# A written first-stage order made anew, and conversion stages dealt to slots by a table

## The chip, the cores and the metric

One core of a Trainium2 chip runs the whole program. The metric is device time in microseconds (us) of one execution, taken as the median of several runs; less is better. The core has five engines with queues of their own: TensorE (PE; its weight loads are shown apart, PEld), VectorE (DVE), ScalarE (ACT), GpSimd (POOL), and SyncE (SP), whose queue issues the DMA transfers. Each engine takes its instructions in the order in which they were written, and waits when one of them needs something that is not there yet.

## What is computed

Three layers follow one another, cut here to what matters:

```python
# 1. attention, both ways, for 4 batches x 8 heads (512 rows, 32 states, 64 wide)
a  = softmax(0.125 * x @ state.T);   xread = a @ state
a2 = softmax(0.125 * state @ x.T);   sread = a2 @ x
x  = rows of [xread, sread]                   # 2304 x 512
# 2. first layer pair: 2048 wide, leaky, w_in and w_out come as float64
h = x @ w_in;  g = max(h, 0) + alpha * min(h, 0);  x = g @ w_out
# 3. eight experts, 1024 wide, with a gate normalized 8 times by rows and columns
P = exp(x @ w_gate - max);  8 times: P /= rowsum; P /= colsum; P *= N / E
out = sum over e of P[:, e] * (relu(x @ w1[e]) @ w2[e])
```

The result is wanted in float32, so each large product is made of three: every operand is split into a high and a low part (`h`, `l`), and high by high, high by low and low by high are added in PSUM.

## The kernel before

The 2048 columns of layer 2 are cut into eight units of 256. A unit's weights come as four raw pieces of float64. A piece goes through `to_f32`, a generator of three stages: stage 1 takes the exponent field (VectorE `y` L122, ScalarE `raw` L125 and `y` L126), stage 2 puts the mantissa together (VectorE L128, ScalarE L132 and L133, GpSimd sum L134), stage 3 merges the sign (VectorE L136). Then `split_w` makes the high half on ScalarE (L151) and the low half on GpSimd (L152), and `load_next` issues the load of a later raw piece into the buffer that has come free; there are three.

Attention and layer 2 are not kept apart. For the first two units the input side is folded: `v_part` multiplies the small states with the unit's weights (`pv`, L481), and its halves are evicted by ScalarE (L491) and VectorE (L494) into V; `first_layer` multiplies V with the attention weights (`ph`, L567), then come the negative part on ScalarE (L572), the leak on VectorE (L575), the halves on ScalarE (L580) and GpSimd (`gl`, L581); `second_layer` multiplies with w_out (`po`, L599), and an accumulate adds it to `acc` (L612 on VectorE, or a copy on ScalarE for unit 0).

The order of this first stage is written out by hand in `PLAN`, a list of 280 steps; `start` takes one step of the named generator for each word:

- `x0` to `x3`: `read_x`, the forward attention of a batch: scores `psc` (L257, 8 narrow products of 64 columns each, 16 records, for each half), softmax on VectorE, ScalarE and GpSimd, transposes `pat` (L289) and `pst` (L301).
- `s0` to `s3`: `read_state`, the other direction: transposes `pa` (L326), products `psr` (L335).
- `cUJ`: the conversion of piece J of unit U; `vUPJ`: a `v_part`; `hUCF`, `oUCD`: layer 1 and layer 2 blocks of unit U; `tB`: halves of a state; `b`: a constant.
- `w`: five idle products of `ones` by `ones` (`warm`, L1318, 10 records, since each float32 product is recorded twice), read by nobody.

All engines but SP run this list in the order in which it was written. Behind it, `run` walks through the remaining units: `program` alternates layer 1 of one chunk with layer 2 of the chunk before, and after each block `slot()` gives every lane of helper work one turn; a unit has 28 slots, and a block of six products of 512 columns fills one. The lane `w` holds `weights(u + 1)`, which converts the next unit's pieces while unit u is multiplied, and the lane `v` makes V as soon as the first two pieces are split. A generator that yields k is left alone for k slots. The last two units are interleaved, and there the code takes the rest of `weights(7)` at once, ahead of unit 7's first block:

```python
if (u, c) == (U1 - 1, 0):
    while (u, NPIECE - 1) not in split:
        advance("w")
```

The third layer (`experts`) follows with an order of its own, from about 412 us on.

Of the kernel before, what the change touches and what calls it, by code (L numbers as in the profile page):

```python
# [39 lines left out]
EPS = 1e-9  # L40
CUT = (1, 2, 0)
PLAN = """
c00 x0 t0 x0 c00 x1 w x0 x0 t1 x0 x0 x0 c01 x1 c02 x0 c00 s0 c01
c02 x0 x0 c01 c00 c01 t3 x0 x0 t2 x1 s0 x1 c02 v001 v000 s0 v001 c02 s0
v000 c03 s0 x1 v010 s0 x1 x1 x1 b c03 c10 h000 v010 c03 w c10 s0 x1 h000
c03 v011 v011 s1 x1 h001 c11 x1 x1 s1 x2 x2 w h000 c11 x2 x2 s1 x2 x2
x2 s1 x2 c10 h011 s1 c12 h001 h001 s1 c10 h011 c11 x2 h011 h010 s1 h010 c12 o002
x2 c11 h010 x2 o001 x2 x3 o001 x3 o003 o002 c13 o013 x3 x3 s2 x3 x3 o013 v101
x3 o003 o011 o011 v100 v101 o000 o000 s2 c12 v100 c13 v110 h101 x3 c13 o010 h101 c12 v110
c13 h100 h110 h100 h110 h101 v111 s2 h100 o010 o012 s2 h111 v111 h111 s2 h021 o102 s2 h110  # L50
o012 o100 o102 h111 h020 x3 o101 o100 h021 s2 o111 o110 s3 o101 h020 c20 o111 c20 o110 x3
o103 h020 h121 h021 x3 s3 h120 o103 x3 o112 s3 h120 c21 h121 o021 s3 o021 c22 o023 h030
c21 o023 o112 s3 c20 o113 h121 s3 o022 h030 o113 h120 h031 o022 c22 o020 o123 h031 s3 o122
o020 h031 c21 h030 h131 o121 h040 c20 o123 o122 o121 c21 c22 h131 h130 o120 h130 o030 o120 v201
o032 h131 o030 c23 h040 v201 h040 h130 o032 o033 v211 o033 o031 h140 o131 h040 o130 o031 o131 c23
v211 o040 o130 h140 c23 v210 v210 v200 o041 o041 c22 o132 o040 h140 o133 v200 o132 c23 h140 o133
"""
SCALE = 0.125

# [2 lines left out]
def body(ctx: ExitStack, tc: tile.TileContext, xt_in, xn_in, stb, stk, wd, ws, alpha, wgate, out):  # L62
# [8 lines left out]
    first = ExitStack()  # L71
# [10 lines left out]
    def f32(t):  # L82
        return t.bitcast(F32)
# [18 lines left out]
    def load_w(u, j):  # L102

        raw_t[u, j] = rawp.tile([P, 512], U64, tag="raw", name=f"raw{u}_{j}")
        nc.sync.dma_start(out=raw_t[u, j], in_=wd[u, j])

    def load_next(u, j):

        i = u * NPIECE + j + 3
        if i < U1 * NPIECE:  # L110
            load_w(i // NPIECE, i % NPIECE)

    def to_f32(u, j):

        w = raw_t[u, j].bitcast(I32).rearrange("p (n two) -> p n two", two=2)
        s = raw_t[u, j].bitcast(U16).rearrange("p (n four) -> p n four", four=4)
        lo_w, hi_w = w[:, :, 0], w[:, :, 1]  # L120
        y = rawp.tile([P, 512], F32, tag="y", name=f"y{u}_{j}", bufs=2)
        nc.vector.tensor_scalar(  # L122
            out=y.bitcast(I32), in0=hi_w, scalar1=16, scalar2=0x7FFF, op0=ALU.logical_shift_right, op1=ALU.bitwise_and
        )
        nc.scalar.activation(out=lo_w, in_=lo_w.bitcast(U32), func=AF.Copy, scale=2.0**-29)  # L125
        nc.scalar.activation(out=y, in_=y.bitcast(I32), func=AF.Relu, bias=rebias)  # L126
        yield
        nc.vector.scalar_tensor_tensor(  # L128
            out=lo_w, in0=s[:, :, 2], scalar=8.0, in1=lo_w, op0=ALU.mult, op1=ALU.add
        )  # L130

        nc.scalar.activation(out=y, in_=y, func=AF.Relu, scale=-1.0, bias=full)  # L132
        nc.scalar.activation(out=y.bitcast(I32), in_=y, func=AF.Copy, scale=-float(1 << 19), bias=4095.0 * (1 << 19))  # L133
        nc.gpsimd.tensor_tensor(out=lo_w, in0=y.bitcast(I32), in1=lo_w, op=ALU.add)  # L134
        yield
        nc.vector.scalar_tensor_tensor(  # L136
            out=lo_w, in0=hi_w, scalar=-0x80000000, in1=lo_w, op0=ALU.bitwise_and, op1=ALU.bitwise_or
        )
        src_t[u, j] = f32(lo_w)

    def split_w(u, j):
        if j % 2 == 0:

            for x, w in zip("hl", (wh_t, wl_t), strict=True):
                t = wp.tile([P, 2, 512], F32R, tag=("ws", "w2")[j // 2] + x, name=f"w{x}{u}_{j}")
                w[u, j], w[u, j + 1] = t[:, 0], t[:, 1]
                if j == 0:
                    w[u] = t
        split.add((u, j))
        src = src_t[u, j]  # L150
        nc.scalar.activation(out=wh_t[u, j], in_=src, func=AF.Copy)  # L151
        nc.gpsimd.tensor_tensor(out=wl_t[u, j], in0=src, in1=f32(wh_t[u, j]), op=ALU.subtract)  # L152
# [1146 lines left out]

    def weights(u, converted=0, first=5):  # L1300

        yield first
        for j in range(NPIECE):
            if j >= converted:
                for _ in to_f32(u, j):
                    yield 2
                yield 1
            split_w(u, j)
            load_next(u, j)
            yield 1  # L1310

    warm_ps = ps_o.tile([P, P], F32, tag="o", name="warm")
# [64 lines left out]
    def run(program):  # L1377
        for kind, u, c in program:
            if kind == 1:
# [11 lines left out]
                if c == 0 and 2 <= u < U1 - 1:  # L1391
                    lanes["w"].append(weights(u + 1, 0, 0 if u == U1 - 2 else 1))
                    lanes["v"].append(make_v(u + 1))
# [162 lines left out]
```

## Time and profile before

| | us |
|---|---|
| median of 3 runs | 1828.98 (1828.03 to 1837.77) |
| the profiled execution | 1835.02 |
| its span, first to last instruction | 1833.2 |
| TensorE busy | 1779.6 (97%) |
| VectorE busy | 1507.6 (82%) |
| GpSimd busy | 1250.8 (68%) |
| ScalarE busy | 736.9 (40%) |
| chain that ended last, on TensorE | 69% |

The page gives busy shares over the whole span; a stretch can look quite different. The views below are the windows (busy time of every engine in a stretch, with the granted clock of TensorE as a share of 2.4 GHz, so that 0.50 is 1.2 GHz and values between are a mix), the timeline of one engine (each line a run of like instructions, with the idle time before it and what ended it in brackets), and the waits (who waited for whom, with the total, the number of times and the longest). Products overlap on TensorE, so what a product costs is the distance from its start to the next one's, not its duration.

### The profile page before, as it was taken

How to read it: one execution, taken by the hardware profiler on the slowest of the kernel's cores; microseconds unless marked ns; L12 is line 12 of the kernel's file. 1: busy time of each engine (PE TensorE's matmuls, PEld its weight loads, DVE VectorE, ACT ScalarE, POOL GpSimd, SP SyncE). 2: the span in 40 equal slices, each digit the busy share in tenths (PEclk: the TensorE clock that was granted, in tenths of full speed). 3: DMA queues.
4: the chain of work that ended last, by engine and by line, in shares of the span. 5: the costliest groups of instructions: out<-in, count | busy, mean ns of one | idle time of the engine just before them, and what ended most of it. 6: DMA issues, size and time to landing. Idle time of an engine off the chain costs nothing.

```text
span 1833.2 us, 28679 instructions
## 1 busy us (share of the span) xinstructions
PE 1779.6 (97%) x9893; PEld 1649.8 (90%) x9893; DVE 1507.6 (82%) x2317; ACT 736.9 (40%) x1386; POOL 1250.8 (68%) x1289
## 2 busy tenths in 40 slices
PE   7999999899999999999999999999999999999998
PEld 7888888678888888888889999999999999999998
DVE  6656788776999999999987777777788888788777
ACT  6767667644234334433332222222223233232332
POOL 4345555566667777776747777777776898777775
PEclk8899999999999999999999999999999999999999
DMA  5211111114568898888887777677777787988884
GB/s 202 69 53 58 58 47 58 43 67 173 218 243 328 331 326 310 315 320 309 293 305 290 256 269 262 250 258 253 261 275 256 270 307 275 334 297 305 314 306 158
DMA packets 153008, 427.16 MB, mean 233 GB/s; under 512 B 17296, under 2 KB 34192, under 8 KB 152864
## 3 DMA queue, kind: packets, MB, share of 16 engines
q1 hardware_dynamic: 152864, 425.34, 64.0%
q8 instruction: 79, 1.29, 0.3%
q14 instruction: 65, 0.53, 0.1%
HBM read 302.28 MB, written 122.99 MB: 232 GB/s over the span
## 4 chain that ended last, share of the span: by engine, by line
PE 69%; DVE 16%; DMA 4%; issue 4%; POOL 4%; ACT 3%; SPq 1%; DVEq 0%; POOLq 0%; ACTq 0%
PE pm L1074 23%; PE py L901 11%; PE px L901 7%; PE pz L901 7%; PE po L599 7%; PE po L1219 4%; PE ph L567 4%; DVE oa L1241 2%; DVE wz L851 2%; DVE g2l L924 2%; PE psc L257 1%; DVE c L908 1%; POOL w2l L723 1%; DMA kept_bs<-wz 1%; DMA kept_a_h<-wah 1%
## 5 line engine op out<-in xcount | busy, mean ns | idle before, releaser
L1080 DVE TENSOR_TENSOR m<-pm,m 128x768 f32<-128x768 f32 (+1 forms) x427 | 377.6, 886 | 125.0 <-PE pm L1074 124.8
L1074 PE MATMUL pm<-formgh,wz 128*128 128x384 f32 (+1 forms) x1134 | 212.6, 322 | 0.4 <-DVE m L1080 0.4
L1005 POOL TENSOR_TENSOR formgh<-mid,formgh 128x384 fp32r<-128x384 f32 (+1 forms) x126 | 121.2, 962 | 105.2 <-ACT formgh L1004 105.1
L901 PE MATMUL px<-rB,wah 128*128 128x384 f32 (+1 forms) x768 | 188.8, 328 | 3.6 <-DVE g2l L924 3.4
L901 PE MATMUL py<-rT,wsh 128*128 128x384 f32 (+1 forms) x768 | 188.5, 328 | 2.3 <-DVE u L908 2.3
L1074 PEld LDWEIGHTS pm<-formgh,wz 128*128 128x128 f32 x1134 | 186.7, 188 | 0.7 <-issue 0.7
L723 POOL TENSOR_TENSOR w2l<-rw,w2h 128x512 fp32r<-128x512 f32 x64 | 87.3, 1385 | 128.9 <-ACT w2h L721 118.9
L923 ACT ACTIVATE g2h<-c 128x384 fp32r<-128x384 f32 x96 | 50.5, 526 | 305.5 <-DVE c L908 305.5
L1219 PE MATMUL po<-w2l,g2h 128*128 128x512 f32 x384 | 153.1, 399 | 0.0
L1219 PE MATMUL po<-w2h,g2h 128*128 128x512 f32 x384 | 152.3, 397 | 0.0
L1219 PE MATMUL po<-w2h,g2l 128*128 128x512 f32 x384 | 150.7, 392 | 0.1
L901 PEld LDWEIGHTS px<-rB,wah 128*128 128x128 f32 x768 | 135.8, 188 | 11.6 <-DVE g2l L924 5.8
L901 PEld LDWEIGHTS py<-rT,wsh 128*128 128x128 f32 x768 | 136.0, 188 | 5.7 <-DVE u L908 2.7
L1015 POOL TENSOR_TENSOR T<-mid,mid 128x384 f32<-128x384 f32 (+1 forms) x126 | 118.1, 960 | 30.8 <-DVE mid L989 29.5
L1004 ACT ACTIVATE formgh<-mid 128x384 fp32r<-128x384 f32 (+1 forms) x126 | 63.0, 500 | 176.6 <-DVE mid L989 135.0
L1241 DVE SCALAR_TENSOR_TENSOR oa<-po,pr,oa 128x512 f32<-128x512 f32 x168 | 124.2, 739 | 9.8 <-PE po L1219 9.2
L581 POOL TENSOR_TENSOR gl<-r,gh 128x512 fp32r<-128x512 f32 x64 | 86.8, 1364 | 61.1 <-ACT gh L580 39.1
L989 DVE SCALAR_TENSOR_TENSOR mid<-mid,pb 128x384 f32<-128x384 f32 (+1 forms) x192 | 122.7, 639 | 6.6
L901 PE MATMUL py<-rT,wsl 128*128 128x384 f32 (+1 forms) x384 | 125.7, 327 | 0.0
L1074 PE MATMUL pm<-formgl,w2h 128*128 128x384 f32 (+1 forms) x504 | 121.2, 323 | 4.5 <-POOL formgl L1005 2.7
L901 PE MATMUL px<-rB,wal 128*128 128x384 f32 (+1 forms) x384 | 125.3, 326 | 0.0
L1015 POOL TENSOR_TENSOR formgl<-T,formgl 128x384 fp32r<-128x384 f32 (+1 forms) x126 | 121.5, 964 | 1.6 <-ACT formgl L1022 1.5
(251 smaller groups left out, 5084.5 us busy)
## 6 DMA issues: line engine op xcount, KB each, us to landing
wz<-kept_bs SPq DMA_DIRECT2D x126, 512.0 KB, 8.1
kept_bs<-wz SPq DMA_DIRECT2D x64, 512.0 KB, 5.9
wsh<-kept_as_h SPq DMA_DIRECT2D x64, 512.0 KB, 3.6
wsl<-kept_as_l SPq DMA_DIRECT2D x64, 512.0 KB, 5.9
wah<-kept_a_h SPq DMA_DIRECT2D x64, 384.0 KB, 2.9
wal<-kept_a_l SPq DMA_DIRECT2D x64, 384.0 KB, 4.2
w2h<-kept_b_h SPq DMA_DIRECT2D x63, 384.0 KB, 6.4
w2l<-kept_b_l SPq DMA_DIRECT2D x63, 384.0 KB, 7.0
```

The source lines that it names most:

```text
L567: nc.tensor.matmul(ps, lhsT=w, rhs=x, start=(i == 0), stop=(i == len(terms) - 1))
L581: nc.gpsimd.tensor_tensor(out=lo, in0=r, in1=f32(hi), op=ALU.subtract)
L599: nc.tensor.matmul(bank, lhsT=w, rhs=x, start=first_of, stop=last_of)
L723: nc.gpsimd.tensor_tensor(out=lo[:, i], in0=src[:, i], in1=f32(hi[:, i]), op=ALU.subtract)
L901: nc.tensor.matmul(bank[b], lhsT=w[:, k * P:(k + 1) * P], rhs=xf[:, j, k, :], start=(first and i == 0), stop=(i == 5), skip_group_check=True,)
L989: nc.vector.scalar_tensor_tensor(out=out, in0=src, scalar=0.0, in1=pb[:, e % 2, h * n:(h + 1) * n], op0=ALU.max, op1=ALU.mult)
L1005: nc.gpsimd.tensor_tensor(out=lo, in0=out, in1=f32(hi), op=ALU.subtract)
L1015: nc.gpsimd.tensor_tensor(out=out, in0=x, in1=y, op=ALU.subtract)
L1074: nc.tensor.matmul(ps[:, q, :n], lhsT=w[:, q * P:(q + 1) * P], rhs=x, start=(j == 0), stop=(j == 2))
L1080: nc.vector.tensor_tensor(out=mm[g][name], in0=ps[:, :, :n], in1=mm[g][name], op=ALU.add)
L1219: nc.tensor.matmul(ps, lhsT=x[:, f, t * P:(t + 1) * P], rhs=w[:, f, :], start=(i == 0), stop=(i == 3 * NF - 1))
L1241: nc.vector.scalar_tensor_tensor(out=a, in0=ps, scalar=p, in1=a, op0=ALU.mult, op1=ALU.add)
```

## The change

`PLAN` is another list of the same steps: each word stands in it as often as before, but for `w`, of which there are 7 instead of 3. Two rows of the 17 show its form:

```diff
-c00 x0 t0 x0 c00 x1 w x0 x0 t1 x0 x0 x0 c01 x1 c02 x0 c00 s0 c01
+w w t0 x0 x0 w x0 t1 c00 x0 x0 x0 w x0 c01 w s0 x0 w x1
...
-v211 o040 o130 h140 c23 v210 v210 v200 o041 o041 c22 o132 o040 h140 o133 v200 o132 c23 h140 o133
+v201 h140 o131 o121 o133 c22 h040 v201 o132 o133 v210 o040 c23 o041 o132 o130 h140 c22 v210 o130
+c23 o041 o040 h140
```

`weights`, which serves units 3 to 7, now fills a table `due` from slot numbers to functions and walks through it one slot at a time. Within a piece the stages stand at slots 0, 2 and 5 (before: 0, 2 and 4), the split at slot 7 (before: 5), which is slot 1 of the next piece; a piece still begins every six slots. `converted` is 0 in every call. `first` is 1, and 0 for unit 7; before, `yield 0` and `yield 1` began at the same slot, in the table 0 begins one slot earlier.

```diff
     def weights(u, converted=0, first=5):

-        yield first
+        due, at = {}, first
         for j in range(NPIECE):
             if j >= converted:
-                for _ in to_f32(u, j):
-                    yield 2
-                yield 1
-            split_w(u, j)
-            load_next(u, j)
+                stages = to_f32(u, j)
+                for k in (0, 2, 5):
+                    due[at + k] = lambda stages=stages: next(stages, None)
+                at += 6
+            else:
+                at += 1
+
+            def last(j=j):
+                split_w(u, j)
+                load_next(u, j)
+
+            due[at + 1 if j >= converted else at - 1] = last
+        for t in range(max(due) + 1):
+            if t in due:
+                due[t]()
             yield 1
```

Since lines were added, line numbers of the kernel after are higher by 1 from `PLAN` on and by 11 behind `weights`. In the rows below, names carry the program's buffer numbers behind the last underscore.

TensorE at the head of the list (`psc` scores, `warm` idle products, `pat` and `pst` transposes, `pv` V). Before:

```order
L257 MATMUL psc_0_147<-xt_0_108 128x64 x8
L257 MATMUL psc_1_160<-xt_0_108,xt_1_111 128x64 x8
L257 MATMUL psc_0_173<-xt_0_124 128x64 x8
L1318 MATMUL warm<-ones 128x128 x5
L257 MATMUL psc_1_212<-xt_0_124,xt_1_127 128x64 x8
L289 MATMUL pat_0_247<-ident,early_101 128x128 x4
L289 MATMUL pat_1_254<-ident,early_101 128x128 x4
L301 MATMUL pst_0_276<-ident,sc_0_191 128x128 x2
L301 MATMUL pst_0_276<-ident,sc_1_201 128x128 x2
L301 MATMUL pst_1_285<-ident,sc_0_191 128x128 x2
```

After:

```order
L1329 MATMUL warm<-ones 128x128 x10
L258 MATMUL psc_0_157<-xt_0_108 128x64 x8
L258 MATMUL psc_1_166<-xt_0_108,xt_1_111 128x64 x8
L1329 MATMUL warm<-ones 128x128 x20
L258 MATMUL psc_0_235<-xt_0_124 128x64 x8
L290 MATMUL pat_0_254<-ident,early_101 128x128 x4
L290 MATMUL pat_1_261<-ident,early_101 128x128 x4
L258 MATMUL psc_1_280<-xt_0_124,xt_1_127 128x64 x8
L302 MATMUL pst_0_297<-ident,sc_0_192 128x128 x2
L302 MATMUL pst_0_297<-ident,sc_1_198 128x128 x2
```

Ten idle products now stand ahead of the first scores and twenty behind the first two score blocks, where one run of five stood behind the third; the fourth score block has moved behind `pat`.

VectorE in a plain unit, the same place in each of units 2 to 5 (`r` the leak, `raw` the merge of stage 3, `acc` an accumulate, `y` stage 1). Before:

```order
L575 SCALAR_TENSOR_TENSOR r_1_0_1928<-r_1_0_1928,beta,ph_1_0_1921 128x512
L136 SCALAR_TENSOR_TENSOR raw_0_1657<-raw_0_1657 128x512
L575 SCALAR_TENSOR_TENSOR r_1_1_1938<-r_1_1_1938,beta,ph_1_1_1931 128x512
L612 TENSOR_TENSOR acc_708<-po_0_0_1942,acc_708 128x512
L122 TENSOR_SCALAR y_1_1968<-raw_1_1754 128x512
```

After:

```order
L576 SCALAR_TENSOR_TENSOR r_1_0_1948<-r_1_0_1948,beta,ph_1_0_1941 128x512
L576 SCALAR_TENSOR_TENSOR r_1_1_1958<-r_1_1_1958,beta,ph_1_1_1951 128x512
L137 SCALAR_TENSOR_TENSOR raw_0_1701<-raw_0_1701 128x512
L613 TENSOR_TENSOR acc_591<-po_0_0_1961,acc_591 128x512
L123 TENSOR_SCALAR y_1_1982<-raw_1_1796 128x512
```

The merge now stands behind the second leak instead of between the two.

VectorE ahead of unit 7's first block (`v` the eviction of V, `raw_3` and `y_3` the last piece). Before:

```order
L575 SCALAR_TENSOR_TENSOR r_2_0_3183<-r_2_0_3183,beta,ph_2_0_3176 128x512
L494 TENSOR_TENSOR v_767<-pv_0_0_3187,v_767 64x512
L494 TENSOR_TENSOR v_766<-pv_0_0_3187,v_766 64x512
L136 SCALAR_TENSOR_TENSOR raw_2_2957<-raw_2_2957 128x512
L575 SCALAR_TENSOR_TENSOR r_2_1_3203<-r_2_1_3203,beta,ph_2_1_3196 128x512
L494 TENSOR_TENSOR v_766<-pv_0_1_3216,v_766 64x512
L494 TENSOR_TENSOR v_767<-pv_0_1_3216,v_767 64x512
L122 TENSOR_SCALAR y_3_3236<-raw_3_3066 128x512
L128 SCALAR_TENSOR_TENSOR raw_3_3066<-raw_3_3066 128x512
```

After:

```order
L576 SCALAR_TENSOR_TENSOR r_2_0_3203<-r_2_0_3203,beta,ph_2_0_3196 128x512
L137 SCALAR_TENSOR_TENSOR raw_2_2995<-raw_2_2995 128x512
L576 SCALAR_TENSOR_TENSOR r_2_1_3214<-r_2_1_3214,beta,ph_2_1_3207 128x512
L495 TENSOR_TENSOR v_667<-pv_0_0_3217,v_667 64x512
L495 TENSOR_TENSOR v_666<-pv_0_0_3217,v_666 64x512
L123 TENSOR_SCALAR y_3_3236<-raw_3_3100 128x512
L495 TENSOR_TENSOR v_666<-pv_0_1_3245,v_666 64x512
L495 TENSOR_TENSOR v_667<-pv_0_1_3245,v_667 64x512
L129 SCALAR_TENSOR_TENSOR raw_3_3100<-raw_3_3100 128x512
```

The second leak and the first step of the last piece have moved ahead, each by one eviction of V; from the `raw_3` row of L128 on the order of VectorE is the same in both, and that of the other engines from this place on as well.

## Rows read from the trace of the kernel before

**Rows 1.** Windows: PE, PEld, DVE, ACT, POOL busy (instructions), granted clock, DMA share, GB/s.

```profile
30.00:84.40 54.40, 47.86 (x253) 42.72 (x253) 36.73 (x66) 38.56 (x72) 20.83 (x17) 0.75 0.25 81
84.40:162.10 77.70, 77.70 (x425) 66.26 (x424) 45.11 (x84) 54.95 (x107) 30.19 (x25) 1.00 0.14 45
```

**Rows 2.** Timeline of TensorE, front: start, us, operation, operands, count, idle before.

```profile
5.03 3.65 PE L257 MATMUL psc<-xt 128*128 128x64 f32 x16 [5.03 <-DMA xt<-in_xt_dram]
8.47 3.62 PE L257 MATMUL psc<-xt,xt 128*128 128x64 f32 x16
...
15.30 2.45 PE L1318 MATMUL warm<-ones 128*128 128x128 f32 x10
17.54 3.51 PE L257 MATMUL psc<-xt,xt 128*128 128x64 f32 x16
...
27.17 0.58 PE L481 MATMUL pv<-wl,sth 128*128 128x256 f32 x1 [1.89 <-ACT early L307]
```

**Rows 3.** Timeline of TensorE, dense part of the list.

```profile
103.26 1.89 PE L335 MATMUL psr<-a2s,xn 128*128 128x64 f32 x16
104.96 0.48 PE L599 MATMUL po<-gl,wh 128*128 128x512 f32 x1
...
106.43 0.40 PE L567 MATMUL ph<-al,ah 128*128 128x512 f32 x1
...
107.82 0.60 PE L289 MATMUL pat<-ident,early 128*128 128x128 f32 x4
108.17 0.48 PE L599 MATMUL po<-gl,wh 128*128 128x512 f32 x1
```

**Rows 4.** Windows of 10 us, columns as in rows 1.

```profile
30.00:40.00 10.00, 7.22 (x33) 6.55 (x33) 9.43 (x16) 9.08 (x16) 3.81 (x4) 0.67 0.28 96
...
50.00:60.00 10.00, 8.04 (x42) 7.50 (x42) 5.49 (x14) 7.32 (x14) 2.55 (x2) 0.69 0.18 54
...
70.00:80.00 10.00, 9.16 (x58) 7.99 (x58) 5.88 (x10) 7.87 (x17) 5.63 (x5) 0.89 0.46 159
80.00:90.00 10.00, 10.00 (x45) 8.55 (x45) 4.58 (x10) 5.71 (x14) 1.05 (x1) 0.77 0.00 0
```

**Rows 5.** Timelines of ScalarE, VectorE, TensorE: V's evictions, first layer-1 block.

```profile
29.05 2.41 ACT L491 ACTIVATE ah<-pv 64x512 fp32r<-64x512 f32 x4
...
30.27 2.81 DVE L494 TENSOR_TENSOR al<-pv,ah 64x512 fp32r<-64x512 f32 x4 [1.51 <-ACT ah L491]
...
39.15 0.77 PE L567 MATMUL ph<-al,ah 128*128 128x512 f32 x1
```

**Rows 6.** Waits of SP's queue, 0 to 160: total us, times, longest.

```profile
SPq L105 <- POOL wl L152: 62.6, 10, 20.4
SPq L231 <- PE psr L335: 57.5, 12, 16.6
```

**Rows 7.** Timeline of VectorE in a unit; waits of TensorE, 160 to 345.

```profile
211.75 1.78 DVE L136 SCALAR_TENSOR_TENSOR raw<-raw 128x512 int32<-128x512 int32 x1 [0.90 <-POOL raw L134]
...
214.10 0.68 DVE L612 TENSOR_TENSOR acc<-po,acc 128x512 f32<-128x512 f32 x1
...
PE po L599 <- DVE acc L612: 3.1, 5, 0.6
PE po L599 <- POOL gl L581: 1.1, 4, 0.3
```

**Rows 8.** Last units: windows, timelines of TensorE, VectorE and GpSimd.

```profile
345.00:372.00 27.00, 21.86 (x91) 17.15 (x90) 17.48 (x25) 16.40 (x28) 17.18 (x18) 0.87 0.18 68
...
354.02 0.60 PE L567 MATMUL ph<-ah,v 128*128 128x512 f32 x1 [1.85 <-DVE v L494]
...
366.57 0.50 PE L599 MATMUL po<-gl,wh 128*128 128x512 f32 x1 [3.10 <-DVE acc L612]
...
360.35 0.69 DVE L136 SCALAR_TENSOR_TENSOR raw<-raw 128x512 int32<-128x512 int32 x1 [4.26 <-POOL raw L134]
...
359.01 1.30 POOL L134 TENSOR_TENSOR raw<-y,raw 128x512 int32<-128x512 int32 x1 [3.81 <-ACT y L133]
```

More of the change, by code (lines that the diff above doesn't have):

```diff
@@ L42 @@
 PLAN = """
-c00 x0 t0 x0 c00 x1 w x0 x0 t1 x0 x0 x0 c01 x1 c02 x0 c00 s0 c01
[L44 to L55, printed above, removed]
@@ L56 @@
-v211 o040 o130 h140 c23 v210 v210 v200 o041 o041 c22 o132 o040 h140 o133 v200 o132 c23 h140 o133
+w w t0 x0 x0 w x0 t1 c00 x0 x0 x0 w x0 c01 w s0 x0 w x1
+c00 c01 x0 x0 c02 c01 c00 c00 x1 c01 c02 x0 x0 x1 x1 s0 s0 x1 x1 x1
+v001 x1 v000 v001 w c03 v000 c02 x1 b c03 h001 x1 c02 s0 h001 t2 h000 h001 x1
+x1 h000 h010 c03 h000 s0 c10 s0 c03 c10 c11 x2 h011 h010 c10 c11 h011 s0 c11 o000
+o002 x2 o003 h010 t3 h011 c10 s1 o002 c11 x2 x2 o000 s1 x2 v010 x2 o003 s1 o001
+x2 v010 o013 s1 v101 x2 s1 o010 o013 o001 v101 v100 s1 c12 c13 v100 h100 h100 x2 c13
@@ new lines @@
+h101 s1 h101 o012 h100 c12 v011 o010 h110 v011 c12 c13 h101 x2 o011 c12 x2 h110 h111 o012
+x2 c13 h110 h021 x3 h111 x3 h111 o011 s2 o102 x3 x3 s2 x3 o101 x3 h020 s2 o102
+v111 s2 x3 o101 o110 x3 c21 v111 o103 h020 s2 o100 o110 x3 x3 c21 o111 h021 h020 c20
+o100 s2 h030 h021 o111 o103 c22 x3 h031 s2 o023 s3 o023 o113 x3 o113 s3 h031 h030 o021
+v110 o021 s3 o112 s3 o020 h030 o020 o112 o022 h031 v110 c20 h121 h120 o032 o022 h121 s3 c21
+s3 h121 o031 h120 o030 h120 o031 o032 s3 o123 h131 h040 c20 o123 c20 o030 h131 h130 c21 h130
@@ L57 @@
+o033 h131 c22 o122 h130 o033 o120 o120 h040 v200 o122 v200 v211 h140 h040 c23 v211 o121 c23 o131
+v201 h140 o131 o121 o133 c22 h040 v201 o132 o133 v210 o040 c23 o041 o132 o130 h140 c22 v210 o130
+c23 o041 o040 h140
 """
```

## The prediction

> **What bounds the kernel now.** TensorE does, nearly everywhere: it is busy 97% of the span, and the chain that ended last lies on it for 69%. So I read the views in this order: busy time by stretch, to find where TensorE is not at its peak; its timeline there; then who it waits for. In the written list's second half, 84.4 to 162.1, it is busy all of 77.7 us at a granted clock of 1.00; in 30 to 84.4 it is busy 47.86 of 54.4 us, at a mean clock of 0.75 [rows 1]. This clock is a mix of two levels, 1.2 and 2.4 GHz: it is 0.67 to 0.89 in the slices of 10 us shown between 30 and 90 [rows 4]. The same work shows both: 16 products of a score block take 3.44 us from 5.03 to 8.47 [rows 2] and a block of the same shape (`psr`) 1.70 us from 103.26 to 104.96 [rows 3].
>
> The stretch 0 to 30 shows a recorded clock of 1.00, yet the score blocks there start 3.44 us apart, twice the 1.70 [rows 2, 3]. I go by the durations: TensorE is at 1.2 GHz from its first product at 5.03. The Trainium skill (TensorE: Matmul & The Clock Gate, Part 1) says that recorded clock events can be unreliable and are to be cross-checked; the durations here agree. By the recorded clock instead, idle products in front could bring nothing, the first-stage term below would shrink by 1.7 us, and the time would be 1817.
>
> What the first 84.4 us would be at full rate, from the order of before: 12 blocks of 16 narrow products (8 score, 4 `psr`) at 1.70 are 20.4; 16 groups of four transposes at 0.35 (107.82 to 108.17) are 5.6; 3 runs of idle products (10 records, 2.24 us at the low level, half of that 1.12) are 3.4; 4 V blocks of six 256-wide products at half of a 512-wide one, 0.70, are 2.8; 7.2 blocks of six 512-wide products at 1.39 (106.43 to 107.82) are 10.0 [rows 2, 3]. That is 42.2 us of work in 79.4 us: 37 us lost to the low clock and to waits. It is the ceiling of what the new list can win; behind 84.4 there is nothing to win.
>
> **The first stage's list.** The multiset of steps is the same, but for four more `w`, each 10 records. What moves: two `w` stand in front of everything, four more behind the first two score blocks, the seventh behind the first V blocks. The scores of batch 2, which stood together with a `w` (a stretch at 0.69 in 50 to 60 [rows 4]), are parted by dense blocks, and so is the state read of batch 0, which before stood ahead of the first layer-1 block at 39.15 [rows 5].
>
> Front: `ones` is written before TensorE could start, so two `w` (20 records at 0.224) run from about 1.05 to 5.5. They lie in the wait for the first load, 5.03 us [rows 2], and cost 0.5. If they raise the clock, the two score blocks take 1.70 each and end at 8.9; if not, 3.44 each, 12.4. Before, they ended at 11.9, and the first V product came at 27.17, 15.3 us later [rows 2], through ScalarE, VectorE and GpSimd: softmax, two conversions, two splits. The new list has the same conversions in that chain, so I keep 15.3: V at 24.2 or 27.7. Forty records of idle products (4.5 to 9.0 us) lie in that span and hide there as long as they end by about 19.
>
> From V to the first layer-1 product, evictions of V set the pace: four on ScalarE, 2.41 us, four on VectorE, 2.81 us, ending 5.9 us behind the first V product [rows 5]. The new list puts the softmax of batch 1's second half and a second scaling ahead of them: three more ScalarE steps (0.60 each) and some 4 us on VectorE, half of it beside ScalarE's. I take 2 us more, 7.9. The first layer-1 block then starts at 32.1 or 35.6; I take the middle, 33.9.
>
> By then the new list has done 4 score blocks (6.8), 7 `w` (7.8), 5 transpose groups (1.75) and 2 V blocks (1.4): 17.8 us. All of the stage is 42.2 + 77.7 + 4 x 1.12 = 124.4, so 106.6 us are left. Were TensorE at full rate without waits, the stage would end at 140.5 instead of 162.1. Two things are added. The clock is low when layer 1 starts, since TensorE has waited for the evictions: between 0 and 6.8 us at half rate, so 0 to 3.4 lost; 2.0 taken. And waits: following the new order by hand over its next 25 us (ScalarE 0.60, VectorE 0.70, GpSimd 1.30 a step [rows 5, 8]) I find 2.45 us in which a PSUM bank is not yet free: 0.75 ahead of batch 2's first score block, 0.3 ahead of its second, 1.4 ahead of the V block behind it. That is 10%, and I take it for all 106.6, 10.7 us; 5% and 15% are the ends, as the old list shows 6.5 of 54.4 us (12%) and nothing in 77.7 [rows 1]. SP's queue I count at nothing: in the old list its weight loads wait 62.6 us for splits and its state-read loads 57.5 us for TensorE [rows 6], in one queue. The new list sets unit 1's last two weight loads ahead of loads of batch 1's state read, so these now wait for a split that ends at some 44; their reader comes behind 55. Without that cover a late load costs a wait of some 4 us, inside the 15%. Sum: 33.9 + 106.6 + 2.0 + 10.7 = 153.2, against 162.1: **-8.9** (ends -18 and -0.5: 32.1 + 106.6 + 0 + 5.3, and 35.6 + 106.6 + 3.4 + 16.0).
>
> **The table for conversion stages.** A piece still takes six slots, but its third stage comes one slot later, its split two. In a unit, VectorE's merge `raw` (L136) stood ahead of the second leak and of an accumulate; it waited 0.90 us for GpSimd and took 1.78, and the accumulate behind it let TensorE wait 0.60 us [rows 7]. Now the leak goes first, while GpSimd finishes, and the accumulate follows 0.6 us earlier: that wait closes. On GpSimd the second `gl` goes ahead of `wl`, which helps the wait for `gl`. In 160 to 345 all such waits of TensorE are 3.1 and 1.1 us [rows 7]. The splits move by two slots, some 2.8 us, but V of the next unit was finished eight slots ahead of its reader and is now six ahead: free. I take **-2.5**, ends 0 and -4.2. The next weight load waits for the split that frees its buffer, so it issues two slots later on SP's queue; nothing else of the plain units stands behind it there, and with three buffers at six slots a piece it has a piece's time in hand.
>
> **The last unit.** With `first` at 0 the table starts at once, so unit 7's pieces come a slot earlier than before relative to the others. TensorE waits 1.85 us for V, then 3.10 for an accumulate; that accumulate stands behind a merge on VectorE at 360.35, which waited for GpSimd's sum at 359.01, the end of the last piece's forced chain. In 345 to 372 TensorE is busy 21.86 of 27 us at a clock of 0.87 [rows 8]. Now the last piece's first VectorE step stands ahead of V's second pair instead of behind it, some 3 us earlier, and the chain behind it, by steps of 0.6, 0.7 and 1.3, ends 2.0 us earlier. V's own pair comes 0.6 later for it. So 1.85 becomes 2.45 and 3.10 becomes 0.5 to 0.7: -2.0. If the shorter wait keeps the clock up, half of 7 us at the low level (13% of 27 us, twice), 3.5, comes on top; I take 1.0 of it. **-3.0**, ends -6.6 and +1.0 (V's delay with nothing gained). All order behind it is unchanged, and time gained ahead of it passes through, since TensorE bounds what follows.
>
> **Sum.** -8.9 - 2.5 - 3.0 = -14.4. The profiled execution took 1835.0 (span 1833.2), 6.0 above the median of 1829.0; the terms are differences, so 1820.6 on its scale and **1815** on the median's. Ends: -28.8 gives 1800, +0.5 gives 1830.
>
> **Rivals.**
> The idle products do not raise the clock. For it: the one run of them at 15.30 stands between score blocks, and the V products at 27.17 were still slow [rows 2]. Against: there they were 2.2 us, here 9 in a row. Then the forty records end at 21.4, scores, transposes and scores again at 32.1, V follows at 34.7 and layer 1 at 42.6, 8.7 later than taken; one more low spell of 6.8 us costs 3.4: 1815 + 12.1 = 1827.
>
> Slower than before: the clock falls again in the new list's waits. In the old list each fall cost a wait of some 2 us and some 10 us at the low level (0.69 in 50 to 60, 0.77 in 80 to 90 [rows 4]), 2 + 5 = 7 us. My sum holds 12.7, nearly two such spells. It decides from the third spell above these: 1815 + 21 = 1836, four give 1843. For it: each of the new list's blocks of narrow products is followed by a bank that must come free. Against: they are single and stand between dense blocks, as in 84.4 to 162.1, where the clock held.
>
> The list brings nothing: its waits only move, first layer-1 block early but evictions late, and TensorE reaches the first plain unit at 162 as before. Then the last two terms remain: 1823.5.
>
> **How the numbers follow.** Forecast with its ends 0.60; idle products without effect 0.14; nothing from the list 0.14; slower by falls of the clock 0.12. The range reaches from the good end nearly to the third spell: 1801 to 1832. About 9 us, 0.5%, is what a measurement of this kernel can tell from no change: below 1820 lie most of the forecast and a little of the rivals, 0.65; within, 0.26; above 1838, 0.09.
>
> **What would show it.** Right: the first score blocks 1.7 us apart, V at 24 to 28, layer 1 from 32 to 36, the first plain unit (`ph` of unit 2, 162.1 before) at 145 to 160, TensorE waits in the units near nil, 366.57's wait below 1. Wrong: score blocks 3.4 apart behind the `w`, granted clocks of 0.5 between 50 and 100, or a wait for V that grew in each unit.

## The result, and the profile after

| | before | after |
|---|---|---|
| median, us | 1829.27 (1828.03 to 1837.77) | 1808.0 (1805.84 to 1813.12) |
| the profiled execution | 1835.02 | 1807.65 |
| its span | 1833.2 | 1805.6 |
| TensorE busy | 1779.6 (97%) | 1763.6 (98%) |
| VectorE busy | 1507.6 (82%) | 1512.3 (84%) |
| GpSimd busy | 1250.8 (68%) | 1252.9 (69%) |

The ratio of the times is 0.9878 (95% interval 0.9842 to 0.9914): faster by 1.2%. The forecast was 1815, range 1801 to 1832. The direction and the range held; the gain was forecast as 14 us and is 21.

A window of the first stage shows where most of it lies (columns as in [rows 1]):

```profile
30.00:84.40 54.40, 52.83 (x319) 45.26 (x320) 40.70 (x74) 48.46 (x98) 29.27 (x26) 0.97 0.32 98
```

In 30 to 84.4, where TensorE was busy 47.86 us at a clock of 0.75 [rows 1], it is now busy 52.83 at 0.97. Two single slices of 10 us:

```profile
30.00:40.00 10.00, 9.92 (x54) 8.21 (x54) 8.48 (x14) 9.43 (x20) 4.94 (x6) 0.83 0.15 53
...
50.00:60.00 10.00, 9.87 (x57) 7.99 (x57) 7.22 (x16) 9.53 (x19) 6.08 (x6) 1.00 0.34 105
```

The slice from 50 to 60 stood at 0.69 before [rows 4]; it is at 1.00, and so is every other one from 40 on to the stage's end. The slices from 20 to 30 and from 30 to 40, at 0.83 each, still hold a short spell at the low level. TensorE's front, as a timeline:

```profile
1.05 4.63 PE L1329 MATMUL warm<-ones 128*128 128x128 f32 x20 [1.05 <-DVE full L1371]
5.48 2.45 PE L258 MATMUL psc<-xt 128*128 128x64 f32 x16
7.76 1.95 PE L258 MATMUL psc<-xt,xt 128*128 128x64 f32 x16
9.55 4.68 PE L1329 MATMUL warm<-ones 128*128 128x128 f32 x40
14.07 1.90 PE L258 MATMUL psc<-xt 128*128 128x64 f32 x16
...
23.70 0.58 PE L482 MATMUL pv<-wl,sth 128*128 128x256 f32 x1 [4.24 <-POOL wl L153]
...
30.07 0.67 PE L290 MATMUL pat<-ident,early 128*128 128x128 f32 x4 [2.04 <-DVE al L495]
30.45 0.72 PE L568 MATMUL ph<-al,ah 128*128 128x512 f32 x1
```

The idle products start at 1.05. The first score block takes 2.28 us (5.48 to 7.76), the second 1.79; they stood 3.44 apart in [rows 2]. The forty idle products are at full rate, 4.52 us for 40. Then TensorE waits 4.24 us for the first split weight, V starts at 23.70 (27.17 before), and the first layer-1 block at 30.45 (39.15 before [rows 5]). From there to the first plain unit at 142.96 (162.09 before) these are all the waits of TensorE (total us, times, longest):

```profile
PE pst L302 <- DVE al L238: 1.1, 1, 1.1
PE pst L302 <- DVE al L495: 0.3, 1, 0.3
```

In a plain unit VectorE now runs the merge behind both leaks; the pair of lines that answers to [rows 7]:

```profile
190.28 1.41 DVE L576 SCALAR_TENSOR_TENSOR r<-r,beta,ph 128x512 f32<-128x512 f32 x2 [2.02 <-ACT r L573]
191.94 1.77 DVE L137 SCALAR_TENSOR_TENSOR raw<-raw 128x512 int32<-128x512 int32 x1 [0.25 <-POOL raw L135]
193.63 0.68 DVE L613 TENSOR_TENSOR acc<-po,acc 128x512 f32<-128x512 f32 x1
```

The merge waits 0.25 us for GpSimd (0.90 before) and the accumulate comes 1.69 us behind the merge's start instead of 2.35. In the last units, TensorE's waits that answer to [rows 8]:

```profile
333.28 0.50 PE L568 MATMUL ph<-al,v 128*128 128x512 f32 x1 [2.43 <-ACT v L492]
...
334.70 0.79 PE L568 MATMUL ph<-ah,v 128*128 128x512 f32 x1 [0.69 <-DVE v L495]
...
344.24 0.50 PE L600 MATMUL po<-gl,wh 128*128 128x512 f32 x1 [0.77 <-DVE acc L613]
```

The wait of 3.10 us for an accumulate is now 0.77; the wait for V, 1.85, is now 2.43 and 0.69. One of the waits from 281 to 355.3 is new in size (total us, times, longest); it was 0.3 before:

```profile
PE po L600 <- POOL gl L582: 1.5, 1, 1.5
```

The stretch from the first plain unit to the state read of unit 7, 217.1 us before (162.09 to 379.18), takes 212.2 (142.96 to 355.20). From the end of layer 2 on no gain is left: the last layer takes 1415.4 us before and 1413.6 after, and 1413.3 in the second profile of the kernel before that is shown below.

### The profile page after: what moved, and what is told of

Its sections match the earlier page's. It is cut to its first block, busy times and chain, and to the rows that moved or that the text cites. A ratio compares the mean times of both kernels' runs of the same rounds, so it can differ in the third digit from the quotient of the medians.

```text
span 1805.6 us, 28756 instructions
## 1 busy us (share of the span) xinstructions
PE 1763.6 (98%) x9933; PEld 1636.4 (91%) x9933; DVE 1512.3 (84%) x2317; ACT 733.3 (41%) x1386; POOL 1252.9 (69%) x1289
## 4 chain that ended last, share of the span: by engine, by line
PE 74%; DVE 13%; POOL 4%; issue 3%; ACT 3%; DMA 2%; SPq 0%; DVEq 0%; POOLq 0%; ACTq 0%
PE pm L1075 23%; PE py L902 12%; PE po L600 9%; PE px L902 8%; PE pz L902 8%; PE po L1220 5%; PE ph L568 4%; DVE oa L1242 2%; DVE wz L852 1%; POOL w2l L724 1%; DVE g2l L925 1%; PE pv L482 1%; POOL wsl L724 1%; DVE c L909 1%; POOL wal L724 1%
## 5 line engine op out<-in xcount | busy, mean ns | idle before, releaser
L1016 POOL TENSOR_TENSOR T<-mid,mid 128x384 f32<-128x384 f32 (+1 forms) x126 | 118.0, 959 | 30.8 <-DVE mid L990 29.9
```

What stands on the lines that cost most here:

```text
L1016: nc.gpsimd.tensor_tensor(out=out, in0=x, in1=y, op=ALU.subtract)
```

## The experiments

Marks of the profiled executions, in us, read from TensorE's timeline: the first V product, the first layer-1 block, the first plain unit (U2), the last product of unit 7's state read (S7), the first product of the last layer (X).

| kernel | V | layer 1 | U2 | U2 to S7 | S7 to X |
|---|---|---|---|---|---|
| before | 27.17 | 39.15 | 162.09 | 217.1 | 38.6 |
| before, second profile (e5) | 25.06 | 37.04 | 156.52 | 217.1 | 38.5 |
| after | 23.70 | 30.45 | 142.96 | 212.2 | 36.8 |
| list alone (e1) | 23.72 | 30.46 | 142.92 | 217.1 | 36.8 |
| table alone (e2) | 25.58 | 37.56 | 160.40 | 212.3 | 36.8 |
| no idle products (e3) | 26.20 | 33.70 | 146.94 | 212.3 | 36.9 |
| old order, more idle products (e4) | 26.64 | 37.32 | 151.70 | 217.1 | 36.8 |
| no idle products in front (e6) | 27.67 | 34.42 | 147.15 | 212.2 | 36.8 |
| gap ahead of V filled (e7) | 23.65 | 30.45 | 142.87 | 212.3 | 36.8 |

### The two halves of the change apart

e1 is the kernel before with the new list; e2 is the kernel after with the old one.

```diff
 # e1: the kernel before
-PLAN = (the list of before)
+PLAN = (the list of after)
```

> The new list with the old generator of conversions. Theory (the list gives nearly all, because TensorE has neither low spells nor waits in it): the first plain unit starts at 143 us, as in the changed kernel, instead of 162, and the units and the last unit keep their old waits (about 5 us more than in the changed kernel), so 1812. Rival (the table carries more than its waits show, since on the medians only 21 us were won and 19 of them lie in the list of one profile): 1817 or more.

```diff
 # e2: the kernel after
-PLAN = (the list of after)
+PLAN = (the list of before)
```

> The old list with the new table. Theory: first plain unit at 162 us as before; the waits of 0.6 us for an accumulate in the units gone, the wait of 3.1 us in the last unit below 1; 3 to 5 us less than before, 1825. Rival (the table gives nothing that lasts, its gain is given back by longer waits for V): 1829. Rival (the table carries a third of the gain): 1821.

Beside a median of 1828.88 for the kernel before, e1 took 1812.62 (ratio 0.9908, 0.9894 to 0.9923) and e2 1823.97 (0.9972, 0.9962 to 0.9982): -16.3 and -4.9, together -21.2, where the whole change brings -21.3. The halves add up within the spread of the runs, and no closer, since 1.8 us (the last section below) come with either half. The marks say: the list moves U2 and leaves U2 to S7 at 217.1, the table shortens that stretch by 4.9 us and leaves U2 where the old list puts it. The rival "the list brings nothing" is out.

### The kernel before, once more

The trace on which I built the sum was of an execution 6 us above the median, so the same kernel was profiled again.

```diff
 # e5: no line changed
```

> The kernel before once more, for a second profile of its own. Theory (where the low spells fall depends on where the clock's transitions lie against the start, so one profile of before is one draw of several): the profile's first plain unit starts up to 6 us earlier than 162.1, with other low spells, and the time spreads by 5 us or more over runs. Rival (the first profile was slower elsewhere, or its recording cost it): first plain unit at 162 within 1 us, and the 6 us lie behind it.

Beside 1827.87 it took 1825.09 (0.999, 0.9974 to 1.0005), its profiled execution 1827.26. U2 lies at 156.52, 5.6 us earlier than in the first trace, and X comes 5.6 earlier too. V comes 2.1 us earlier already; the rest lies in a window in which the clock was low for less time (columns as in [rows 1]):

```profile
30.00:84.40 54.40, 50.20 (x282) 44.66 (x281) 37.10 (x69) 40.58 (x78) 21.47 (x17) 0.80 0.25 78
```

0.80 here, 0.75 in [rows 1]. Its timeline shows how the clock is lost in the old list:

```profile
48.54 1.29 PE L301 MATMUL pst<-ident,sc 128*128 128x128 f32 x8 [0.78 <-DVE al L494]
50.98 3.42 PE L257 MATMUL psc<-xt 128*128 128x64 f32 x16 [1.15 <-ACT early L307]
54.19 3.62 PE L257 MATMUL psc<-xt,xt 128*128 128x64 f32 x16
57.61 2.45 PE L1318 MATMUL warm<-ones 128*128 128x128 f32 x10
...
61.55 0.40 PE L567 MATMUL ph<-ah,al 128*128 128x512 f32 x1
```

Up to the one at 47.36 the 512-wide products are 0.23 apart, full rate. Then come eight transposes behind a wait of 0.78 and a wait of 1.15 ahead of the next score block, and that block and the one behind it take 3.21 and 3.42 us: the engine has fallen to 1.2 GHz (the granted clock of the slice from 50 to 60 is 0.56) and stays there till some 61.5, where 512-wide products are 0.23 apart again. The waits cost 1.9 us, the low level half of 10, some 5. Over the whole window from 30 to 84.4 the low clock takes at most 10.9 us in e5 (54.4 at 0.80) and 1.6 in the kernel after (at 0.97), and TensorE is idle for 4.2 and 1.6 us: an estimate from these two rows, by which most of what the list gains in this window is the clock.

### What the idle products do

```diff
 # e3: the kernel after, all seven w taken out of the list; its first rows
-w w t0 x0 x0 w x0 t1 c00 x0 x0 x0 w x0 c01 w s0 x0 w x1
+t0 x0 x0 x0 t1 c00 x0 x0 x0 x0 c01 s0 x0 x1
```

> The changed kernel without any of its seven runs of idle products; nothing else is left out. Theory (the idle products raise the clock in front): score blocks start 3.4 us apart, first V at 27 us instead of 23.7, first plain unit 3 to 6 us later than 143, so 1812 to 1815. Rival (the order alone does it, the clock rises by itself as soon as the work is dense): first V within 1 us of 23.7, 1808. Rival (without them the clock falls again and again): first plain unit at 155 or later, 1820.

1812.58 (0.9908, 0.9895 to 0.9922), beside 1808.0 with them: 4.6 us, of which the marks show 4.0 at U2. The timeline:

```profile
5.08 3.65 PE L257 MATMUL psc<-xt 128*128 128x64 f32 x16 [5.08 <-DMA xt<-in_xt_dram]
8.52 3.62 PE L257 MATMUL psc<-xt,xt 128*128 128x64 f32 x16
...
34.27 0.63 PE L567 MATMUL ph<-ah 128*128 128x512 f32 x1
34.70 0.63 PE L567 MATMUL ph<-ah,al 128*128 128x512 f32 x1
...
38.90 0.39 PE L567 MATMUL ph<-ah,al 128*128 128x512 f32 x1
39.13 0.39 PE L567 MATMUL ph<-al,ah 128*128 128x512 f32 x1
```

The engine is at the low level from 5.08 (a score block of 3.44, and 512-wide products still 0.43 apart at 34.27) to some 38.5, where 512-wide products come 0.23 apart. And from there on it holds full rate without a single idle product, through the two waits of 0.3 and 1.1 us that the kernel after has as well. So what keeps the clock up behind the front is the order, not the idle products; they only shorten the low stretch at the beginning. That stretch of 33 us puts U2 off by only 4.0; TensorE waits in it for other engines as well (1.31 us for the first split weight, 3.83 for V's eviction).

```diff
 # e6: the kernel after without the two w in front
-w w t0 x0 x0 w x0 t1 c00 x0 x0 x0 w x0 c01 w s0 x0 w x1
+t0 x0 x0 w x0 t1 c00 x0 x0 x0 w x0 c01 w s0 x0 w x1
```

> The changed kernel without the two runs of idle products ahead of everything; the other five stay. Theory: score blocks of the first batch 3.4 us apart, the chain to V starts at 12 instead of 9.5 but the four runs behind it raise the clock, V at 26.5 to 27.5, first plain unit 2 to 4 us later, 1811. Rival (the front is hidden by what follows): no change of the first plain unit, 1808.

In the same set of runs as e5, 1809.72 (0.9901, 0.9883 to 0.9919). By the medians the two are worth 1.7 us as they stand and 3.1 when each kernel is held against the kernel before of its own set (18.2 us and 21.3 under it), by the mark U2 4.2; runs of this kernel spread by 5 us, so the mark is the better measure, and the medians do not contradict it. The timeline:

```profile
8.70 3.62 PE L258 MATMUL psc<-xt,xt 128*128 128x64 f32 x16
12.12 6.48 PE L1329 MATMUL warm<-ones 128*128 128x128 f32 x40
18.44 1.90 PE L258 MATMUL psc<-xt 128*128 128x64 f32 x16
```

Without them the second score block takes 3.42 us, V comes at 27.67 and layer 1 at 34.42. That is no better than with no idle products at all: in e3 the third score block starts at 11.93 instead of 18.44, V comes at 26.20, and U2 lies at 146.94 beside 147.15. By the marks, then, the five other runs gain nothing without the two in front; the two in front alone were not tried.

```diff
 # e7: the kernel after, four more w ahead of the first V block
-v001 x1 v000 v001 w c03 v000 c02 x1 b c03 h001 x1 c02 s0 h001 t2 h000 h001 x1
+w w w w v001 x1 v000 v001 w c03 v000 c02 x1 b c03 h001 x1 c02 s0 h001 t2 h000 h001 x1
```

> The changed kernel with four more runs of idle products ahead of the first V products, where TensorE waits 4.2 us for a split and where its clock falls. Theory (the low spell of 20 to 33 us costs half of the busy time in it): V's products start 0.12 instead of 0.21 us apart, the first plain unit starts 1 to 2 us earlier, 1806.5, which only the profile can tell. Rival (the evictions set the pace there, not TensorE): first plain unit within 0.5 us of 143. Rival (the products end behind the split): V later by up to 1 us and so is the rest.

1809.14 (0.9902, 0.9885 to 0.9919): nothing gained. The timeline says why:

```profile
19.21 4.63 PE L1329 MATMUL warm<-ones 128*128 128x128 f32 x40
...
30.01 0.79 PE L290 MATMUL pat<-ident,early 128*128 128x128 f32 x4 [3.55 <-DVE al L495]
```

The products fill the 4.24 us ahead of V, V's products are now 0.12 apart instead of 0.21, and all of that is waited for behind them: 3.55 us instead of 2.04 for V's eviction on VectorE. Layer 1 starts at 30.45 in both. Here the chain of splits and evictions sets the pace.

```diff
 # e4: the kernel before, its order kept, w added in three places (9 in all)
-c00 x0 t0 x0 c00 x1 w x0 x0 t1 x0 x0 x0 c01 x1 c02 x0 c00 s0 c01
-c02 x0 x0 c01 c00 c01 t3 x0 x0 t2 x1 s0 x1 c02 v001 v000 s0 v001 c02 s0
+w w c00 x0 t0 x0 c00 x1 w w w w x0 x0 t1 x0 x0 x0 c01 x1 c02 x0 c00 s0 c01
+c02 x0 x0 c01 c00 c01 t3 x0 x0 t2 x1 s0 x1 c02 v001 v000 w s0 v001 c02 s0
```

> The old list with idle products at the same places as in the new one: two runs in front, four behind the first two score blocks instead of one behind the third, one behind the first V; old generator. Theory: the front gains as in the changed kernel (score blocks 1.7 us apart, V at about 24), but the low spells of 54 to 64 and 78 to 84 and the waits stay, so the first plain unit starts at 155 to 158 and the time is 1823. Rival (the idle products are the main cause): first plain unit at 146 or earlier, 1812. Rival (they only delay what stands behind them): 163, 1830.

1824.91 (0.9981, 0.9968 to 0.9993): 4 us under the kernel before, of which 1.8 lie behind S7. e1, the new order with the same old generator, took 12.3 us less in the same set of runs, and the new order without idle products gains 11.4 (16.3 in e3, of which 4.9 are the table's). The profiled execution was the fastest of its runs (1818.26), so its U2 at 151.70 flatters it. It shows the old order with hardly a loss of clock, where the low spells had been expected to stay:

```profile
30.00:84.40 54.40, 47.80 (x313) 41.76 (x312) 43.78 (x78) 46.96 (x89) 23.63 (x19) 0.97 0.25 78
```

```profile
50.64 2.00 PE L258 MATMUL psc<-xt 128*128 128x64 f32 x16 [1.16 <-ACT early L308]
```

The clock of this window is 0.97, as in the kernel after, but TensorE is idle for 6.6 us of it instead of 1.6, and U2 comes 8.7 us later. Most of that, 6.9, is there when layer 1 starts, at 37.32: in the old order evictions and a state read stand ahead of it, whatever the clock. And at the place where e5 loses the clock this execution keeps it: the score block behind the wait of 1.16 us takes 1.83 (the next starts at 52.47). So a wait of that length behind eight transposes does not always bring the clock down. Over all traces the orders differ clearly: from 40 to 142 us the granted clock is 0.90, 0.94, 0.91 and 0.98 in the four of the old order (before, e5, e2, e4) and 1.00 in all ten of the new one, whatever their idle products. That the new order keeps the clock is shown; which of its features does it is not.

### What the table does

```diff
 # e11: the kernel after, third stage back at slot 4, split left where it is
-                for k in (0, 2, 5):
+                for k in (0, 2, 4):
```

> The changed kernel with the third stage of a piece back at slot 4 instead of 5, the split left where the change puts it. Theory A: VectorE's merge is what the plain units gain from, so it stands ahead of the second leak again, waits 0.9 us for GpSimd instead of 0.25, and the accumulate's wait of 0.6 returns some five times in units 2 to 5: 2.5 to 4 us above the changed kernel, about 1811. Theory B: the gain comes from the split's later slots (GpSimd's half goes ahead of the split): no more than 1 us above it, 1808 to 1809.

e9 is the kernel after once more, as the yardstick:

```diff
 # e9: no line changed
```

> The changed kernel once more, as the yardstick of this set. Expected 1808 us and about 0.989 of the kernel before, with TensorE's first plain unit near 143 in the trace, unit 7's state read at 355, and the first wait for a half of the leaky result of unit 7's stretch at 1.5 us.

Beside 1829.61 for the kernel before, e9 took 1807.71 (0.9884, 0.9864 to 0.9904) and e11 1808.36 (0.988, 0.9864 to 0.9896). These medians do not tell the two apart. The traces do: U2 to S7 is 212.3 us in e9 and 214.3 in e11. TensorE's waits in 138 us of plain units of e11:

```profile
PE po L600 <- DVE acc L613: 2.5, 4, 0.6
```

It is the accumulate's wait of [rows 7] (there 3.1 us over a longer stretch; in the same 138 us of the kernel before it is 2.5 in four waits as well). In e9 that row is gone from this stretch, and the wait for a `gl` stands at 0.8 in both. So it is the merge's place on VectorE, as the prediction had it, that closes this wait; the later splits, which e11 keeps, do not.

The other variants shift the beginning of unit 7's table, which the change had set one slot earlier than the other units' (`first` 0 instead of 1). e8 and e10 are the same kernel, in two sets of runs.

```diff
 # e8 and e10: unit 7's table one slot later than in the kernel after
-                    lanes["w"].append(weights(u + 1, 0, 0 if u == U1 - 2 else 1))
+                    lanes["w"].append(weights(u + 1, 0, 1))
```

> The changed kernel with the last unit's table begun one slot later, where the old generator began. Theory (in the last unit the earlier begin is what gains): TensorE's wait for an accumulate there is back to 2 to 3 us, 1 to 2 us in all. Rival (the order of the stages gains it, not the begin): within 0.5 us.

> The changed kernel with unit 7's table begun one slot later, as the other units' is, beside the changed kernel itself. Theory A: the earlier begin, which I forecast as part of a gain of 3.0 us, costs, because one of GpSimd's splits then stands ahead of a half that TensorE waits for (1.5 us in the changed kernel's trace, 0.3 at most in the earlier trace of this variant): 2 to 3 us under the changed kernel, about 1805.5. Theory B: the earlier 1805.14 was another chip's scale, and the begin of the table is free: 1808, within 0.7 of the changed kernel.

```diff
 # e12: two slots later than in the kernel after
-                    lanes["w"].append(weights(u + 1, 0, 0 if u == U1 - 2 else 1))
+                    lanes["w"].append(weights(u + 1, 0, 2 if u == U1 - 2 else 1))
```

> The changed kernel with unit 7's table begun two slots later than in it. If what counts is only that GpSimd's split leaves the half of the leaky result in front, it is like one slot later, 1805 to 1806. If each slot moves the last piece's forced chain as I forecast, about 1.0 us a slot, V of unit 7 and the accumulate behind its merge come later and TensorE's waits there (2.4 and 0.8 us in the changed kernel) grow: 1807 to 1809.

e8 took 1805.14 (0.9873, 0.9856 to 0.9889), e10 1806.15 (0.9869, 0.9851 to 0.9886), e12 1807.9 (0.9877, 0.986 to 0.9894), beside 1807.71 for e9 in the set of e10 and e12. U2 to S7 is 211.3, 211.4 and 213.6, beside 212.3. TensorE's waits from 281 to 355.3 in e10:

```profile
PE po L600 <- POOL gl L582: 0.3, 1, 0.3
PE po L600 <- DVE acc L613: 0.3, 1, 0.3
```

And in e12:

```profile
PE po L600 <- DVE acc L613: 4.0, 2, 3.1
```

In e8 and e10 the wait for an accumulate stays away (0.2 and 0.3 us), so the theory of e8 is out; in e12 the wait of 3.1 us of [rows 8] is back. VectorE's timeline in e10 and e12 shows the step that decides it, the last piece's stage 1 (`y`, L123), against V's second pair of evictions. In e10:

```profile
329.84 0.45 DVE L123 TENSOR_SCALAR y<-raw 128x512 int32<-128x512 int32 x1
332.36 1.39 DVE L495 TENSOR_TENSOR v<-pv,v 64x512 fp32r<-64x512 f32 x2 [2.07 <-ACT v L492]
```

In e12:

```profile
328.67 2.81 DVE L495 TENSOR_TENSOR v<-pv,v 64x512 fp32r<-64x512 f32 x4
331.50 0.43 DVE L123 TENSOR_SCALAR y<-raw 128x512 int32<-128x512 int32 x1
```

In e10 (and in the kernel after) the step goes ahead of the second pair, in e12 behind all four. That is the place the prediction named. But the earlier beginning, to which it ascribed this, is not needed: with the old beginning (e10) the step is already ahead. Nor is the later third stage: in e11, with the third stage back at slot 4, the step stands ahead of the second pair as well (331.30 and 334.78) and the wait for an accumulate in these units is 0.3 us. What remains of the edits is the later splits, which bring V later, too; by themselves they were not tried. What the earlier beginning costs is 1.5 us of wait for a `gl` of GpSimd (0.3 in e10). Whether e10's variant is really faster than the change is not settled: 1.6 us by the medians of one set, 0.9 by the traces, with runs of the changed kernel spread from 1805.2 to 1814.0. Its two medians are the lowest of all that ran.

### A gain that neither half was meant to bring

S7 to X is 38.6 and 38.5 us in the two profiles of the kernel before and 36.8 or 36.9 in every other kernel, in e4 too, which has the old order and the old generator. The order of all engines is the same there. In e5, VectorE, GpSimd and TensorE:

```profile
389.50 0.54 DVE L677 TENSOR_TENSOR acc<-acc 128x384 f32<-128x384 f32 x1
...
390.63 1.40 DVE L677 TENSOR_TENSOR acc<-acc 128x384 f32<-128x384 f32 x1
391.95 1.61 DVE L686 TENSOR_TENSOR rB<-acc,rB 128x384 fp32r<-128x384 f32 x1
```

```profile
390.32 2.83 POOL L581 TENSOR_TENSOR gl<-r,gh 128x512 fp32r<-128x512 f32 x2 [3.35 <-ACT gh L580]
```

```profile
394.22 0.50 PE L599 MATMUL po<-gl,wh 128*128 128x512 f32 x1 [3.02 <-DVE acc L612]
```

And in the kernel after:

```profile
371.51 1.39 DVE L678 TENSOR_TENSOR acc<-acc 128x384 f32<-128x384 f32 x1
372.83 0.55 DVE L687 TENSOR_TENSOR rB<-acc,rB 128x384 fp32r<-128x384 f32 x1
```

```profile
371.20 1.28 POOL L582 TENSOR_TENSOR gl<-r,gh 128x512 fp32r<-128x512 f32 x1 [2.29 <-ACT gh L581]
372.98 1.53 POOL L582 TENSOR_TENSOR gl<-r,gh 128x512 fp32r<-128x512 f32 x1 [0.49 <-ACT gh L581]
```

```profile
374.03 0.50 PE L600 MATMUL po<-gl,wh 128*128 128x512 f32 x1 [0.89 <-DVE acc L613]
```

VectorE's steps of 384 columns on two operands take 0.54 us alone (389.50, ahead of the `gl`) and 1.40 and 1.61 while GpSimd's two `gl` run without a pause (2.83 us). In the kernel after the second `gl` waits 0.49 us for its input, one VectorE step slips through in 0.55, the accumulate is done earlier, and TensorE waits 0.89 instead of 3.02. The Trainium skill (SBUF — State Buffer, "SBUF: two separate sides") says that VectorE, with two inputs in SBUF, and GpSimd share a port pair that one of them holds for a whole instruction while the other is blocked; the durations here agree: a long step ends 0.4 us behind the end of the `gl` beside it (371.51 + 1.39 = 372.90 and 371.20 + 1.28 = 372.48), close to the 0.54 it needs alone. Upstream, the first difference behind S7 between VectorE, ScalarE and GpSimd of e5 and of e4 is a sum on GpSimd (L744, at 379.88 us in e5) that waits 0.24 us for a load of raw weights (`rw`) in e5. In the first profile of the kernel before it waits 0.35 us for that load, in the kernel after, e1 and e4 it does not wait. That this wait shifts all that follows up to the two `gl` is likely and was not tried, and why the load lands later is not settled.

## Why the prediction came out as it did

**Front: right.** V was forecast at 24.2 if the idle products raise the clock and 27.7 if not. It is 23.70 with them, 27.67 in e6 without the two in front, and 26.20 in e3 without any. The rival that they have no effect is out: 1.79 us for the second score block. For layer 1 I took 33.9, the middle of 32.1 and 35.6, and it is 30.45. Of the 3.45 us, 1.8 are the choice of a middle between two ends that excluded each other, 0.5 are V's start, and 1.15 are the steps ahead of V's evictions, counted as 7.9 us and measured as 6.75 (23.70 to 30.45). Of the signs that were named for a right forecast, the score blocks and the wait in the last unit came out; V at 23.70, layer 1 at 30.45 and U2 at 142.96 all lie ahead of the spans given for them (24 to 28, 32 to 36, 145 to 160).

**The rest of the list: the term that failed is the wait.** From 30.45 to 142.96 are 112.5 us. Waits are 1.4 of these, where 10.7 were taken: 10% of the work, from 2.45 us that I found when I followed the new order by hand over 25 us. None of the three waits that I found there happened; the two that did, 0.29 and 1.07 us at 72 and 75, are others. Why the walk found them is my reading and was not tried: it put steps of 0.60, 0.70 and 1.30 us one behind another and gave each chain its full length, though TensorE had dense blocks of 1.4 us to spend between them, the first ones at half rate. The low clock at the start costs 1.7 us (10 us at 0.83), 2.0 taken. The work itself, 112.5 less 1.4 and 1.7, is 109.4, 106.6 counted. So -3.45, -9.3, -0.3 and +2.8: -10.25, from 153.2 to 142.95.

**The base: an error that hid half of this one, by luck.** I subtracted the stage's end from 162.09, which belongs to an execution 6 us above the median, and used the difference on the median's scale. e5 has 156.52, so a forecast of 153.2 was a gain of 3.3 us, not 8.9. That 1815 came within 7 us of the result is thus in part luck: held against 156.52, the three terms as worked out add up to 8.8 us, where 21 were measured. A term that is worked out as a time of its own has to be held against the usual end, not against one draw. By the medians the list is worth 16.3 us and the table 4.9, each with the 1.8 of the last section, which no term held; forecast were 8.9 and 5.5.

**Slower by falls of the clock: did not happen.** The rival asked for three spells above the sum; there are two short ones, at V's products from 23.70 on and at the first layer-1 block from 30.45 to some 34.3, and none behind them in this stage. The first costs nothing, as e7 shows. The argument against the rival in the prediction, that the narrow products are single and stand between dense blocks, is not decided: the old order loses the clock in e5 at waits of 0.78 and 1.15 us around eight transposes, the new one holds it through a wait of 1.07 behind 512-wide products, in e3 with no idle product in the list at all, but e4 holds it at the old order's place as well.

**Table in the plain units: right in place and size.** -2.5 forecast; the four waits of 0.6 us, 2.5 in 138 us, are gone, and e11 brings them back. **Last unit:** -3.0 forecast, 4.9 less 2.5 is 2.4. The wait of 3.10 became 0.77 (0.5 to 0.7 forecast), V's 2.43 (2.45 forecast); the wait of 1.5 us for `gl` had not been seen, and the cause named, the earlier beginning, is not needed (e10). The 1.0 us taken for a higher clock is not seen: over the last 29.3 us up to S7 the granted clock is 0.88 and 0.94 in the two profiles of the kernel before and 0.94 and 0.88 in the two of the kernel after (the second is e9), while U2 to S7 is 217.1 in both of the former and 212.2 and 212.3 in the latter. SP's queue cost nothing, as taken: no wait of TensorE for a load stands in any of these stretches.

**The clock of the views.** The prediction went by the durations where the view shows 1.00 in the first 30 us, and it was right to. e3 is the clearest case; its window (columns as in [rows 1]):

```profile
30.00:40.00 10.00, 7.04 (x26) 6.05 (x27) 7.88 (x14) 8.44 (x16) 4.63 (x4) 1.00 0.01 2
```

The view has a clock of 1.00, while in the same slice 512-wide products are 0.43 apart up to 36 and 0.23 from 38.9 on. The trace's first entry on the clock says full rate from 38.8 us on, which agrees with the products; ahead of its first entry there is none, and the view counts that time as 1.00. In the first profile of the kernel before the first entry lies at 30.0. So it was not that a recorded event was wrong, as the prediction took it: there was no entry yet.

## What to carry to other kernels

Where TensorE loses its clock in a written order, try another order of the same steps before idle products: here the order alone was worth 11 to 12 us by the medians and the idle products 4 to 5 on top, and those only as far as no other chain set the pace beside them. That waits among narrow products are what an order has to avoid fits the traces, with one exception, and is not shown. Profile the kernel before twice before a stage's length is used as a base, since low stretches differ from one execution to the next. And when a chain followed by hand shows waits, weigh them against the dense work that lies between before spreading them over a stage as a share.

## What the runs showed of the hardware

The same kernel, executed twice, reached its first plain unit at 162.09 and at 156.52 us, with a mean clock of 0.75 and 0.80 in the same 54.4 us: low stretches come and go without any change of the program, and these 5.6 us compare with a spread of 1818 to 1838 us over the runs of the kernel before. Forty idle products that begin while the engine is fast run at 0.113 us each; in e6, where they follow slow scores, they take 6.32 us (12.12 to 18.44), so the level changes in the middle of them. And where two GpSimd instructions stood 0.49 us apart instead of back to back, with no change of any order there, VectorE was busy for 29.9 us instead of 31.5 between S7 and X, and TensorE's longest wait for it was 2.1 us shorter.
